# Dilated sliding attention and a squared-ReLU FFN on one core: the order of the first batch, other homes for copies and products, and the last tile in two banks

## The chip, the core and the metric

One core of one Trainium2 chip. The metric is the device time of one launch in microseconds, as the median of several runs: 314.54 us for the kernel before (13 runs, 313.2 to 317.0). The profile is of one execution of 314.25 us. Engines: PE is TensorE, DVE is VectorE, ACT is ScalarE, POOL is GpSimd and SP is SyncE. POOL and SP issue transfers here; ACT issues a few at the start.

## The reference

q, k and v have 8 batches, 8 heads, 576 positions and 64 features. Heads 0 to 3 see the last 32 positions. Heads 4 to 7 see those of the last 128 whose distance is a multiple of 4.

```python
scores = scale * np.matmul(q, k.transpose(0, 1, 3, 2))
rel = pos[:, None] - pos[None, :]
mask_plain = (rel >= 0) & (rel < window)
mask_dil = (rel >= 0) & (rel < window * dilation) & (rel % dilation == 0)
...
attn = attn / (np.sum(attn, axis=-1, keepdims=True) + 1e-09)
...
x = np.ascontiguousarray(attn_out.transpose(0, 2, 1, 3)).reshape(B * S, H * D)
h = np.maximum(x @ w_in, 0.0)
return (h * h @ w_out).astype(np.float32)
```

The FFN takes all 4608 tokens from 512 features to 2048 and back.

## The kernel before, in words

**FFN.** It is cut into tiles of tokens: four of 256, then seven of 512. A tile consists of groups of products. A group of the first layer (`mm1`, L655) multiplies quarters of w_in with the transposed attention output xT into a bank of PSUM (L665); ACT applies ReLU into h2T (L676) and DVE squares it (L677). A group of the second layer (`g2`, L692) adds four products of 128 tokens with a quarter of w_out (L700); after the fourth, ACT copies the bank into osb (L706) and SP stores it. Of the last 128 tokens of all, each half of the columns is finished, copied and stored by itself (L696 to L698), both halves in one bank. The first two 512-token steps' products are cut once more by heads (`g1`, L679), so that they can start before the last head pair is ready. FFN groups are numbered from 0 over the whole kernel.

**Attention.** Two heads form a pair, e = 0 to 3; pairs 0 and 1 are the plain ones, 2 and 3 the dilated ones. For each batch and pair, q and k have to be transposed. In batches 0, 1 and part of 2, PE transposes them into PSUM (`trans`, L221, products at L235), and copies (`halves`, L240; L248 for q, L252, L259 and L265 for k) bring them to qT and kbd: four copies for each q or k, two for each head. kbd holds two heads as blocks on a diagonal, so one product does both. Later batches are transposed by transfers (`cross`, L213), and the same copies take them from SBUF. v is spread into vbd by transfers or by DVE (`spread_v`, L202). `scores` (L295) makes products of kbd and qT, ACT takes the exponential (L314), DVE multiplies by the mask (L315). `pv` (L342) multiplies with vbd (L413) and with ones for the sums (L415); ACT makes the reciprocal as logarithm and exponential (L417, L418), and DVE multiplies into xT (L428). PSUM has four banks in pool pf for the FFN, two in pa, and one each in po and pd. Products of batches 0 and 1 with e odd go to pf, all others to po and pd.

**The order** is written by hand in `PROGRAM` (L21). What stands ahead of the first `|` is done before FFN group 0; after FFN group n, the codes of the (n+1)-th part that follows are done. I call that slot n. Slots hold codes of batches 1 to 5; the rest follows a rule. A code such as `1q2` is batch, step and pair. q and k transpose and copy, Q and K do it for a batch's second part (positions from 256 on), v and V spread v, a and b are the two halves of scores, o and p the two halves of products. `L` codes load, and `L3:x` is the transposing transfer.

The first batch has steps of its own (`first_step`, L471), with pair and part as digits: T transposes, C copies (L504 to L512), B adds the mask's bias to PSUM, S the scores (L546), E the exponential (L554) and, in the second part (x1), the mask (L557), P the products with v (L584), D the sums (L600), L and X the reciprocal (L607, L610), M the product into xT (L617). W with a number issues that many products of an idle tile on PE (L467, `turn`).

Of the kernel before, what the change touches and what calls it, by code (L numbers as in the profile page):

```python
# [20 lines left out]
PROGRAM = (  # L21
    "L0:q001 L0:q023 L0:q101 L0:q123 L0:v0d L0:i0 L0:v1dr L0:i1 L0:v1p L0:i2 L0:i3 L0:o0 L0:o1 L0:o2 L0:o3 "
    "L1:q00123 z y L1:v0dp L1:q10123 L1:v1dpr w9 T00 C00a T10 C10a B00 B10 W2 S00 E00 B20 W1 S10 E10 u B30 W3 "
    "T20q W6 T20k C20v T30 C30v h W3 S20 E20 W2 S30 E30 T01 C01v T11 C11v W2 P00 P10 D00 D10 L00 X00 M00 P20 "
    "P30 D20 D30 L20 X20 M20 S01 T21 C21a T31 C31v E01 S11 E11 | S21 E21 | S31 E31 P21 P31 D21 D31 L21 X21 M21 "
    "L31 X31 M31 | | P01 P11 D01 D11 L01 X01 M01 L11 X11 M11 | | | | | | | | | | | | | m n | | | | | L2:q00123 "
    "L2:q10123 | 1q1 1q3 | 1q2 1k2 | 1k1 1v3 | 1a2 | 1v2 1k0 1q0 | 1o2 | 1a0 1a1 | 1k3 1o0 1o1 | 1a3 1Q0 | 1K0 "
    "1o3 | 1Q1 1K1 | 1Q2 | 1b0 | | 1Q3 1K2 L2:vwpdr L3:q00123 L3:q10123 | L2:x | | 2q0 | | 2k0 1V2 | 1b2 1p0 | "
    "1b1 1V3 1K3 | | 1p2 1p1 | 2a0 1b3 | 2k1 2o0 2b0 1p3 | 2q1 2k2 L3:x | | 2q2 2p0 L3:vwpdr 2a1 | | | 2b1 | "
    "2o1 2q3 2a2 | | 2p1 2v2 | 2k3 | 2b2 2o2 | 2v3 | 2a3 2p2 L4:q10123 | 2b3 3k1 | 2o3 3q1 | | 3a1 L4:q00123 "  # L30
    "2p3 | 3k0 3k2 | | 3o1 | | | 3q0 3v2 | | | | 3a0 | 3b1 3k3 | | | 3p1 L4:x 3q2 L4:vwpdr | | 3b0 | 3a2 3q3 "
    "3o0 4k0 | | | 3o2 3b2 | | 3p0 3v3 | 4q1 3a3 | 3p2 4q2 4q0 | L5:q10123 3b3 | 3o3 | 4k1 | | L5:q00123 3p3 "
    "4k2 4k3 4a0 L5:vwpdr | | | 4b0 | | 4q3 | | 4o0 | | | 4a2 4v2 | 4b2 | 4a3 L5:x 4a1 | 4o2 | | | 4p2 "
    "L6:q00123 4v3 | | 4b1 | | 4p0 | | 4p1 | 5q0 5k0 | 4b3 | | | | 4o1 | | 5k2 L6:q10123 4o3 | 5q2 5k1 | | 4p3 "
    "| 5q1 |"
)


# [25 lines left out]
def kernel(  # L64
# [9 lines left out]
    nc = tc.nc  # L74
    P = nc.NUM_PARTITIONS
    B, H, S, D = q.shape
    DM, DFF = moe_w_in.shape
    NTOK = B * S
    assert H * D == DM
    bf16 = mybir.dt.bfloat16  # L80
# [5 lines left out]
    NE = H // 2  # L86
# [3 lines left out]
    M = S // RES  # L90
# [5 lines left out]
    PARTED = (0, 1)  # L96
    STAGE = (0, 1, 0, 2, 2, 2, 0, 1)
    ADDED = 4
# [12 lines left out]
    ps_f = ctx.enter_context(tc.tile_pool(name="ps_f", bufs=4, space=bass.MemoryType.PSUM))  # L111
    ps_a = ctx.enter_context(tc.tile_pool(name="ps_a", bufs=2, space=bass.MemoryType.PSUM))
# [37 lines left out]
    def staged(b: int, nm: str):  # L150


        t = rb[STAGE[b]][nm]
        return t[:, :].rearrange("p (a h x) -> p a h x", h=H, a=2)
# [47 lines left out]
    def spread_v(b: int, e: int, parts):  # L202

        p0, p1 = parts[0], parts[-1] + 1
        for hl in range(2):
            rows = slice(64 * hl, 64 * hl + 64)
            nc.vector.tensor_copy(  # L207
                vbd[b % 2][rows, e, RES * p0 : RES * p1, rows],
                vds[b][rows, e - NE // 2, p0:p1, :].rearrange("p m (r d) -> p (m r) d", d=D),
            )  # L210
# [7 lines left out]
            staged(b, nm)[0:n, part, h0:, :].rearrange("p h x -> p (h x)"),  # L218
        )

    def trans(b: int, e: int, nm: str, part: int):  # L221

        ps = ps_a.tile([P, 1024], bf16, name="pa")
        t = staged(b, nm)
        copy = nc.scalar.copy if nm == "q" and e < NE // 2 else nc.vector.tensor_copy
        if b == 2:
            m0, n, pitch, cuts = 0, M, M, [(t[0:80, a, :, :], MS[a], 80) for a in range(2)]
        else:

            m0, n, pitch, cuts = MS[part], MN[part], 80, [(t[0:80, part, :, :], 0, 80)]  # L230
        pv_ = ps[:, 0 : 4 * pitch].rearrange("p (h c m) -> p h c m", h=2, c=2)
        for hl in range(2):
            for c in range(2):
                for src, c0, w in cuts:
                    nc.tensor.transpose(  # L235
                        pv_[:, hl, c, c0 : c0 + w], src[:, 2 * e + hl, P * c : P * c + P], ident[0:w, 0:w]
                    )
        halves(e, nm, pv_[:, :, :, 0:n], m0, n, copy)

    def halves(e: int, nm: str, t, m0: int, n: int, copy):  # L240


        for hl in range(2):
            rows = slice(64 * hl, 64 * hl + 64)
            for jj in range(2):
                src = t[64 * jj : 64 * jj + 64, hl, :, :]
                if nm == "q":
                    copy(  # L248
                        qT[rows, e, :, m0 : m0 + n].rearrange("p (c j) m -> p j c m", j=2)[:, jj, :, :], src
                    )  # L250
                elif e < NE // 2:
                    copy(  # L252
                        kbd[rows, e, m0 // 16 : (m0 + n) // 16, rows].rearrange(
                            "p i (m c j) -> p j i m c", c=2, j=2)[:, jj, :, :, :],
                        src.rearrange("p c (i m) -> p i m c", m=16),
                    )
                else:
                    x0, x1 = m0 // 64, min((m0 + n) // 64, 2)
                    copy(  # L259
                        kbd[rows, e, RES * x0 : RES * x1, rows].rearrange(  # L260
                            "p (x c j) m -> p j c x m", c=2, j=2)[:, jj, :, :, :],
                        src[:, :, 0 : 64 * (x1 - x0)].rearrange("p c (x m) -> p c x m", m=64),
                    )
                    if m0 + n == M:
                        copy(  # L265
                            kbd[rows, e, 8, rows].rearrange("p (m c j) -> p j m c", c=2, j=2)[:, jj, :, :],
                            src[:, :, n - 16 : n].rearrange("p c m -> p m c"),
                        )
# [163 lines left out]
    def step(b: int, code: str):  # L432

        what, e = code[0], int(code[1])
        part = int(what in "QKVbp")
        if what in "qk" and (b > XB or b == XB and e >= NE // 2):
            t = (qx if what == "q" else kx)[b % 2]
            by_act = what == "q" and e < NE // 2 and b < ADDED  # L440
            halves(
                e, what, t[:, 2 * e : 2 * e + 2, :, :], 0, M, nc.scalar.copy if by_act else nc.vector.tensor_copy
            )
        elif what in "qQkK":
            trans(b, e, what.lower(), part)
        elif what in "vV":
            spread_v(b, e, [part] if b in PARTED else [0, 1])
        elif what in "ab":
            scores(b, e, part)
        elif b in PARTED and e % 2:  # L450
            pv(b, e, part, ps_f, "pf")
        else:
            pv(b, e, part)
# [175 lines left out]
    def store(osb, pos: int, c0: int = 0, c1: int = DM):  # L629

        x = 0
        while x < P:
            b, y = divmod(pos + x, S)
            part = int(y >= RES * MN[0]) if b in PARTED else 0
            w = MN[part] if b in PARTED else M
            r, m = divmod(y - RES * MS[part], w)
            n = min(P - x, w - m)
            row = b * S + RES * (MS[part] + m) + r
            nc.sync.dma_start(out[row : row + RES * (n - 1) + 1 : RES, c0:c1], osb[x : x + n, c0:c1])
            x += n  # L640

    def ffn_groups(tk0: int, nt: int):
# [3 lines left out]
        early = NT <= tk0 <= 2 * NT  # L646
# [43 lines left out]
                mm1(i, kts)  # L690

        def g2(m, part):  # L692
            if part == 0:
                cur[m] = ps_f.tile([P, DM], f32, name="pf")

            last = tk0 + P * (m + 1) == NTOK  # L696
            c0, c1 = (DM // 2 * (part // 2), DM // 2 * (part // 2 + 1)) if last else (0, DM)
            f0, f1 = (NF // 2 * (part % 2), NF // 2 * (part % 2 + 1)) if last else (4 * part, 4 * part + 4)  # L698
            for f in range(f0, f1):
                nc.tensor.matmul(  # L700
                    cur[m][:, c0:c1], h2[:, f, P * m : P * m + P], w_out_sb[:, f, c0:c1],
                    start=(f == 0), stop=(f == NF - 1),
                )
            if f1 == NF:
                osb = osb_pool.tile([P, DM], f32, name="osb")
                nc.scalar.copy(osb[:, c0:c1], cur[m][:, c0:c1])  # L706
                store(osb, tk0 + P * m, c0, c1)

        return [lambda i=i: g1(i) for i in range(NF // per)] + [
            lambda m=m, part=part: g2(m, part) for m in range(nt // P) for part in range(4)  # L710
        ]

# [163 lines left out]
```

## Time and profile before

| | |
|---|---|
| median of 13 runs | 314.54 us (313.2 to 317.0) |
| the profiled execution | 314.25 us, span 312.5 us |
| mean granted clock of PE | 0.995 |
| FFN, first layer (L665) | 768 products, 135.0 us busy |
| FFN, second layer (L700) | 592 products, 134.5 us busy |
| h2T square on DVE (L677) | 144, mean 423 ns |
| ReLU on ACT (L676) | 144, mean 597 ns |

Start and length stand first in a row of the timeline, then engine, line, operation, output and inputs. Busy time of PE overlaps from product to product, since ends are modelled, so late starts are found by the difference of starts. Slots come in time order: slot 22 is at 41.9 us, slot 64 at about 93.9 us.

### The profile page before, as it was taken

How to read it: one execution, taken by the hardware profiler on the slowest of the kernel's cores; microseconds unless marked ns; L12 is line 12 of the kernel's file. 1: busy time of each engine (PE TensorE's matmuls, PEld its weight loads, DVE VectorE, ACT ScalarE, POOL GpSimd, SP SyncE). 2: the span in 40 equal slices, each digit the busy share in tenths (PEclk: the TensorE clock that was granted, in tenths of full speed). 3: DMA queues.
4: the chain of work that ended last, by engine and by line, in shares of the span. 5: the costliest groups of instructions: out<-in, count | busy, mean ns of one | idle time of the engine just before them, and what ended most of it. 6: DMA issues, size and time to landing. Idle time of an engine off the chain costs nothing.

```text
span 312.5 us, 6788 instructions
## 1 busy us (share of the span) xinstructions
PE 303.9 (97%) x2564; PEld 187.4 (60%) x2564; DVE 196.0 (63%) x637; ACT 197.6 (63%) x421; POOL 94.0 (30%) x138
## 2 busy tenths in 40 slices
PE   8989999999999999999999999999999999999994
PEld 4669746968755555555599655555555555445443
DVE  1446568898987879985799469946994334104400
ACT  6658638759878956785388547854686456226511
POOL 8679788626083127401451041000000000000000
PEclk9979999999999999999999999999999999999999
DMA  7999999999999899995699975602200210121022
GB/s 107 196 183 215 199 153 185 196 158 200 142 133 205 110 186 140 142 183 69 93 130 129 163 121 94 103 8 61 67 3 0 69 68 0 36 67 34 2 67 67
DMA packets 79808, 35.04 MB, mean 112 GB/s; under 512 B 49824, under 2 KB 74784, under 8 KB 79776
## 3 DMA queue, kind: packets, MB, share of 16 engines
q0 software_dynamic: 46592, 18.23, 51.0%
q1 hardware_dynamic: 32496, 16.06, 26.4%
q10 hardware_dynamic: 688, 0.33, 0.5%
q8 instruction: 20, 0.33, 0.4%
q14 instruction: 12, 0.10, 0.1%
HBM read 36.90 MB, written 9.44 MB: 148 GB/s over the span
## 4 chain that ended last, share of the span: by engine, by line
PE 85%; ACT 5%; DMA 4%; DVE 2%; issue 2%; POOL 0%; ACTq 0%; POOLq 0%
PE pf L665 38%; PE pf L700 37%; PE po L413 3%; DMA w_in<-in_moe_w_in_dram 3%; PE pd L415 2%; DMA qb<-in_q_dram 2%; PE pa L304 2%; ACT h2T L676 1%; PE pa L310 1%; ACT qT L248 1%; PE pa L235 1%; ACT rec L417 1%; DVE kbd L252 1%; DVE xT L428 1%; ACT rec L418 1%
## 5 line engine op out<-in xcount | busy, mean ns | idle before, releaser
L665 PE MATMUL pf<-xT,w_in 128*128 128x256 bf16 (+1 forms) x768 | 135.0, 328 | 0.9 <-DVE xT L428 0.3
L700 PE MATMUL pf<-w_out_sb,h2T 128*128 128x512 bf16 (+1 forms) x592 | 134.5, 373 | 0.5 <-ACT osb L706 0.5
L665 PEld LDWEIGHTS <-w_in 128*128 128x128 bf16 x768 | 82.7, 114 | 36.9 <-issue 1.2
L676 ACT ACTIVATE h2T<-pf 128x512 bf16<-128x512 f32 x144 | 83.7, 597 | 23.5 <-PE pf L665 22.9
L700 PEld LDWEIGHTS <-h2T 128*128 128x128 bf16 x592 | 54.3, 98 | 54.0 <-issue 0.7
L677 DVE TENSOR_TENSOR h2T<-h2T 128x512 bf16<-128x512 bf16 x144 | 58.0, 423 | 38.7 <-ACT h2T L676 37.1
L706 ACT COPY osb<-pf 128x512 f32<-128x512 f32 (+1 forms) x37 | 21.2, 573 | 43.5 <-PE pf L700 41.3
L428 DVE TENSOR_TENSOR xT<-po,rec 128x288 bf16<-128x288 f32 (+2 forms) x52 | 23.7, 456 | 31.5 <-ACT rec L418 31.0
L178 POOL DMA_DIRECT2D vbd<-in_v_dram x36 | 25.7, 729 | 54.2 <-PE pd L415 49.4
L417 ACT ACTIVATE rec<-pd 128x288 f32<-128x288 f32 (+2 forms) x52 | 21.5, 413 | 24.0 <-PE pd L415 22.9
L314 ACT ACTIVATE pt<-pa 128x352 bf16<-128x352 f32 (+6 forms) x56 | 27.6, 499 | 8.4 <-PE pa L310 4.7
L418 ACT ACTIVATE rec<-rec 128x288 f32<-128x288 f32 (+2 forms) x56 | 24.8, 444 | 1.8
L413 PEld LDWEIGHTS <-vbd 128*128 128x128 bf16 x286 | 16.8, 97 | 10.0 <-DVE vbd L207 0.7
L248 DVE COPY qT<-xx 64x288 bf16<-64x288 bf16 x80 | 19.6, 246 | 1.1
L161 POOL DMA_DIRECT2D qb<-in_q_dram x18 | 13.0, 721 | 21.8 <-DMA xx<-qb 19.6
L252 DVE COPY kbd<-xx 64x288 bf16<-64x288 bf16 x40 | 18.8, 470 | 0.6
L413 PE MATMUL po<-pt,vbd 128*128 128x96 bf16 (+3 forms) x263 | 18.0, 199 | 0.3 <-DVE vbd L207 0.2
L191 POOL DMA_DIRECT2D vd<-in_v_dram x24 | 14.7, 630 | 6.4 <-DMA kb<-in_k_dram 2.6
L415 PE MATMUL pd<-pt,mk 128*128 128x96 bf16 (+5 forms) x158 | 16.3, 204 | 0.0
L161 POOL DMA_DIRECT2D kb<-in_k_dram x18 | 12.8, 712 | 0.4 <-issue 0.3
L304 PE MATMUL pa<-qT,kbd 128*128 128x96 bf16 (+2 forms) x146 | 12.2, 201 | 0.5 <-ACT qT L248 0.5
L197 POOL DMA_DIRECT2D vbd<-in_v_dram x16 | 9.6, 606 | 9.4 <-PE pd L415 7.4
(90 smaller groups left out, 236.7 us busy)
## 6 DMA issues: line engine op xcount, KB each, us to landing
out_dram<-osb SPq DMA_DIRECT2D x18, 128.0 KB, 4.5
qb<-in_q_dram POOLq DMA_DIRECT2D x7, 320.0 KB, 7.7
kb<-in_k_dram POOLq DMA_DIRECT2D x7, 320.0 KB, 9.0
vd<-in_v_dram POOLq DMA_DIRECT2D x32, 64.0 KB, 4.8
w_in<-in_moe_w_in_dram POOLq DMA_DIRECT2D x4, 512.0 KB, 7.8
w_out_sb<-in_moe_w_out_dram POOLq DMA_DIRECT2D x4, 512.0 KB, 11.4
qb<-in_q_dram POOLq DMA_DIRECT2D x7, 256.0 KB, 6.2
kb<-in_k_dram POOLq DMA_DIRECT2D x7, 256.0 KB, 7.5
```

Source lines behind the costliest of these rows:

```text
L161: nc.gpsimd.dma_start(t[0:n, part, hs, :], src[b, hs, t0 : t0 + RES * n, :].rearrange("h (p r) d -> p h (r d)", r=RES))
L178: nc.gpsimd.dma_start(dst[rows, e, i0:i1, rows], v[b, 2 * e + hl, 64 * i0 : 64 * i1, :].rearrange("(i p) d -> p i d", p=64),)
L248: copy(qT[rows, e, :, m0 : m0 + n].rearrange("p (c j) m -> p j c m", j=2)[:, jj, :, :], src)
L314: nc.scalar.activation(pt[:, off : off + n], ps[:, 0:n], ACT.Exp, scale=SCALE)
L413: nc.tensor.matmul(oo, vb[:, e, i, :], rh, start=(x == 0), stop=(x == len(mms) - 1), skip_group_check=True)
L417: nc.scalar.activation(rec[:, 0:n], d[:, 0:n], ACT.Ln)
L418: nc.scalar.activation(rec[:, 0:n], rec[:, 0:n], ACT.Exp, scale=-1.0)
L428: nc.vector.tensor_tensor(out=tok, in0=o if o is o3 else o[:, 0:n], in1=rec if o is o3 else rec[:, 0:n], op=ALU.mult)
L665: nc.tensor.matmul(acc[u][:, nt * x + y0 : nt * x + y1], w_in_sb[piece][:, kt, c0 : c0 + 509 : 4], xT[:, kt, t0 : t0 + y1 - y0], start=(kt ...
L676: nc.scalar.activation(hv, acc[u][:, :].rearrange("p (x n) -> p x n", x=per), ACT.Relu)
L677: nc.vector.tensor_tensor(out=hv, in0=hv, in1=hv, op=ALU.mult)
L700: nc.tensor.matmul(cur[m][:, c0:c1], h2[:, f, P * m : P * m + P], w_out_sb[:, f, c0:c1], start=(f == 0), stop=(f == NF - 1),)
```

## The change

`PROGRAM` has another order in the first batch. The first batch's `T21 C21 T31 C31` move from after S01 to between L00 and X00. S21, S31, E21 and E31, which stood in and behind slots 0 and 1, and S01, S11, E01, E11 all stand before FFN group 0 now, E21 and E31 first. C11 has its q copied by ACT, C21 by DVE. W2 ahead of P00 becomes W4.

```diff
-C20v T30 C30v h W3 S20 E20 W2 S30 E30 T01 C01v T11 C11v W2 P00 P10 D00 D10 L00 X00 M00 P20
-P30 D20 D30 L20 X20 M20 S01 T21 C21a T31 C31v E01 S11 E11 | S21 E21 | S31 E31 P21 P31 D21 D31 ...
+C20v T30 C30v h W3 S20 E20 W2 S30 E30 T01 C01v T11 C11a W4 P00 P10 D00 D10 L00 T21 C21v T31
+C31v X00 M00 P20 P30 D20 D30 L20 X20 M20 S21 S31 E21 E31 S01 S11 E01 E11 | | P21 P31 D21 D31 ...
-L2:q10123 | 1q1 1q3 | 1q2 1k2 | 1k1 1v3 | 1a2 | 1v2 1k0 1q0 | 1o2 | 1a0 1a1 | 1k3 1o0 1o1 | ...
+L2:q10123 | 1q1 1q3 | 1q2f 1k2f | 1k1a 1v3 | 1a2 | 1v2 1k0a 1q0v | 1o2 | 1a0 1a1 | 1k3 1o0 1o1f | ...
-1b1 1V3 1K3 | | 1p2 1p1 | 2a0 1b3 | 2k1 2o0 2b0 1p3 | 2q1 2k2 L3:x | ...
+1b1 1V3 1K3 | | 1p2 1p1f | 2a0 1b3 | 2k1l 2o0 1p3f 2b0 2k1h | 2q1 2k2 L3:x | ...
-2o1 2q3 2a2 | | 2p1 2v2 | 2k3 | 2b2 2o2 | 2v3 | 2a3 2p2 L4:q10123 | 2b3 3k1 | 2o3 3q1 | | 3a1 L4:q00123 2p3 | 3k0 3k2 | | 3o1 | | | 3q0 3v2 |
+2o1 2a2 2v2 2q3 | | 2p1f | 2k3 | 2b2 2o2 | 2v3 | 2a3 2p2f L4:q10123 | 2b3 2o3 | 3k1 | 2p3 | 3q1v L4:q00123 | 3k0l | 3a1 | 3k0h | | 3o1 3k2l | 3q0 | 3k2h 3v2 |
```

A code may now end in its home: `f` puts its PSUM into pool pf, `a` and `v` have its copies done by ACT or DVE, `l` does the first head's two copies and `h` the second head's later. Products go to pf only with an `f`: of those that went there before, 1o3 goes to po and pd now. New are 2p1 and 2p2 in pf.

```diff
-    def trans(b: int, e: int, nm: str, part: int):
-        ps = ps_a.tile([P, 1024], bf16, name="pa")
+    def trans(b: int, e: int, nm: str, part: int, home: str):
+        pool, name = (ps_f, "pf") if "f" in home else (ps_a, "pa")
+        ps = pool.tile([P, 1024], bf16, name=name)
         t = staged(b, nm)
-        copy = nc.scalar.copy if nm == "q" and e < NE // 2 else nc.vector.tensor_copy
+        copy = copier(nm, e, home, True)
...
+    def copier(nm: str, e: int, home: str, early: bool):
+        act = "a" in home or "v" not in home and nm == "q" and e < NE // 2 and early
+        return nc.scalar.copy if act else nc.vector.tensor_copy
...
-        elif b in PARTED and e % 2:
+        elif "f" in home:
             pv(b, e, part, ps_f, "pf")
```

In the last tile, the second half of the columns takes a bank of its own:

```diff
         def g2(m, part):
-            if part == 0:
+            last = tk0 + P * (m + 1) == NTOK
+            if part == 0 or last and part == 2:
                 cur[m] = ps_f.tile([P, DM], f32, name="pf")
```

## The prediction

> **What bounds the kernel now.** I read the page first: busy shares, then the tenths with the clock row.
>
> ```profile
> PE 303.9 (97%) x2564; PEld 187.4 (60%) x2564; DVE 196.0 (63%) x637; ACT 197.6 (63%) x421; POOL 94.0 (30%) x138
> ...
> PE   8989999999999999999999999999999999999994
> ...
> PEclk9979999999999999999999999999999999999999
> ```
>
> TensorE (PE) is never long idle, and from 126 us to 306 us no group of its products starts late. A gain can only come from late starts of PE and from its clock. So I went through the PE timeline with the price of one product: in the chain, 13.81 us for 64 products of 512 columns gives 0.216 us each, and 10.48 us for 96 of 256 columns gives 0.109 us. Where the next start is later than that, PE stood still. These late starts are in three places.
>
> The head. Stages of 3.4 us, columns as in the first line (PE, PEld, DVE, ACT, POOL, clock, DMA share, GB/s), then the chain of waits:
>
> ```profile
> 12.92:16.34 3.42, 2.64 (x75) 2.01 (x76) 1.58 (x3) 3.09 (x6) 2.22 (x4) 1.00 1.31 194
> 16.34:19.75 3.41, 3.41 (x32) 2.31 (x32) 1.74 (x7) 1.50 (x4) 3.30 (x5) 0.50 1.56 187
> 19.75:23.16 3.41, 2.60 (x66) 2.21 (x65) 1.34 (x4) 2.03 (x4) 1.97 (x5) 1.00 1.29 179
> ```
>
> ```profile
> 8.25 7.91 DMA w_in<-in_moe_w_in_dram
> 16.16 0.05 issue
> 16.21 1.83 PE pf L665 x8
> 18.04 0.67 PE pf L546 x9
> 18.71 0.99 PE pf L665 x4
> ...
> 20.75 0.60 ACT pt L554
> 21.35 0.02 issue
> 21.37 0.44 DVE pt L557
> ...
> 21.85 0.59 PE pa L584 x14
> ```
>
> The first weights land at 16.16 us, then FFN groups 0 and 1 run at half clock, then the chain goes over the exponential (L554) and mask (L557) of heads 6 and 7, second part. The third FFN group starts at 22.72 us. The same stretch has 0.89 us in which PE waits for the values (12.71 to 13.60).
>
> The middle. Lines from the PE timeline; the bracket is the idle time before and its releaser:
>
> ```profile
> 43.37 0.30 PE L235 MATMUL pa<-mk,qb 80*128 80x80 bf16 x4 [0.15 <-ACT qT L248]
> ...
> 54.85 0.82 PE L665 MATMUL pf<-xT,w_in 128*128 128x256 bf16 x6 [0.25 <-ACT osb L706]
> ...
> 93.89 0.32 PE L304 MATMUL pa<-qT,kbd 128*128 128x96 bf16 x4 [0.45 <-ACT qT L248]
> ...
> 96.13 1.02 PE L665 MATMUL pf<-xT,w_in 128*128 128x512 bf16 x4 [0.27 <-DVE xT L428]
> ```
>
> The bracket is shorter than the loss, since the modelled ends overlap it. Start to start, less the price of the product, the losses after 40 us are: 0.32 (ends 43.37), 0.18 (44.7), 0.25 (46.9), 0.19 (49.4), 0.42 (54.8), 0.17 (62.3), 0.25 (76.1), 0.26 (83.5), 0.36 (86.2), 0.62 (93.9), 0.43 (96.1), 0.20 (120.6): 3.6 us.
>
> The tail:
>
> ```profile
> 306.48 0.37 ACT L706 COPY osb<-pf 128x256 f32<-128x256 f32 x1 [1.16 <-PE pf L700]
> 306.90 1.91 PE L700 MATMUL pf<-w_out_sb,h2T 128*128 128x256 bf16 x16 [0.51 <-ACT osb L706]
> ```
>
> The last tile's second half waits until ScalarE (ACT) has copied the first half out of the same bank: start to start 0.78 us where 0.11 is due.
>
> **The head, part by part.** W4 for W2 is two more dummy products of 256 columns: 2 x 0.109 = 0.2 us later for P00, P10 and their sums D00, D10, which then end near 13.1. T21 and T31 (32 transposes, 0.8 us by the rows at 14.69 to 15.5) move ahead of P20, into the old wait for the values: they end near 13.8, so P20 starts 0.15 us after those values have landed (it began at 13.30 and 13.65), and ends with its sums at 14.6. VectorE (DVE) now takes C21 and C31 (0.48 + 0.21 us each) from 13.5 to 14.9, so M00 behind them moves from 14.23 to 14.9 and ends at 15.6: it is due at 16.2, so nothing is lost. The copy of T11 by ACT (L511) costs 0.3 us where ACT stood idle (1.41 us before L607). PE then has S21 and S31 (0.5 us each), S01 and S11 (0.3 each) until about 16.3; ACT has, after its reciprocals (to 15.9), E21, E31 (0.6 each), E01, E11 (0.5 each), to 18.1. The accumulators of FFN group 0 are the banks that E21 and E31 free at 16.5 and 17.1: groups 0 and 1 start at 16.5, not at 16.2. Their 16 products end at 18.4 at full clock, at 19.9 at half clock. Masks for heads 4 to 7 are done by then, so P21, P31, D21, D31 (1.3 us from the rows 20.47 to 20.84 and 21.85 to 22.7) follow without the old 0.98 us stop before 21.85, and end at 19.7 or 21.2. The third FFN group needs the second quarter of the weights, issued at 13.22 and landing 7.8 us later, at 21.00. So it starts at 21.05 or 21.2 in place of 22.72: **-1.6 us**, nearly the same at either clock. What is late next: the third quarter (landed 24.28) is due at 24.5, the fourth (27.33) near 30.7, the last quarter of w_out (37.21) near 38.4; all hold.
>
> Here a rule has to be weighed. The Trainium skill, "TensorE: Matmul & The Clock Gate", Part 1, has the clock fall after an idle window of about 3.4 us. The row 12.92:16.34 says otherwise: PE was busy for 2.64 of 3.42 us and the next window still had half clock, while 19.75:23.16, no busier (2.60), kept full clock. By the rule the change would get 18.4 for groups 0 and 1; by the row, with some 0.4 us less idle and 36 more small products in that window, either may come. The sum takes the row, and the weights' landing makes both ends equal to 0.15 us.
>
> **Batch 1 (slots 22 to 35).** The transposes 1q2 and 1k2 go to two of the four banks of pool pf. Those two last held accumulators that ACT read long before, so 1q2 needs no bank of 1q1 and the 0.32 goes. k of pair 1 and 0 is copied by ACT, q of pair 0 by DVE: 8 copies of L252 (0.30 us each on DVE) leave DVE, 4 of L248 (0.22) come. A kbd copy by ACT is nowhere in the trace. Nearest row: ACT's L248 for the same 64x128 takes 0.27 (1.08 for four); the wider L252 on DVE takes 0.47. I take 0.27 to 0.30; the ends are 0.22 and 0.47, worth -0.2 and +0.8 us on each of two chains of four copies. From the start of slot 22 as zero, before had 1a2 at 3.8, 1a0 at 7.55 and 1o3 at 11.7 us; walking the new order with these durations gives 1a2 at 3.5 (q2 and k2 by DVE end at 3.45), 1a0 at 6.7, 1o0 at 8.2 (ACT is now busy with an output copy and a reciprocal ahead of that exponential), 1o3 at 11.0. That gains 0.66, and the 0.42 at 54.8 goes, because one pair of products fewer sits in pf and the late accumulator takes its bank 2.6 us later: **-1.0 us** of 1.36. The product 1o3 moves to the single pair po, pd, which frees 0.9 us before it is due. The 0.17 at 62.3 stays.
>
> **Batches 2 to 4 (slots 45 to 72).** Splitting 2k1 puts two copies (2 x 0.49 us) behind 1p3's product into xT; it frees its bank 0.98 us earlier, and 0.25 goes. 2p1 in pf does not wait for po: 0.26. 2v2 two slots earlier: 0.36. For 3a1, count from T, the end of FFN group 61: DVE does 2o3's product to T+2.5, four copies of 3k1 (0.47 each) to T+4.4, 2p3's product to T+4.9, four of 3q1 (0.25) to T+5.9. Group 66 wants 2p3's result at T+5.2, so the 0.43 goes; 3a1 comes at T+5.6 and waits 0.3, where it was 0.62. Together 0.25 + 0.26 + 0.36 + 0.43 + 0.3 = 1.6. 3q1 is 1.0 us more on DVE in a stretch that was 90% busy (100:110); its last h2T product was ready 1.7 us before its use at 108.5, so it covers that with 0.7 left; without it this costs up to 1.0. I book 0.3 for new small waits: **-1.3 us**. The 0.20 at 120.6 stays.
>
> No load, transposing transfer or store changes place in POOL's or SP's order. PE now runs up to 4 us ahead of transfers which do not move: the tightest is batch 1's first q (landed 38.96, due at 40.3 after the head's gain), then batch 2's q (56.25 against 58.9) and k.
>
> **Tail.** The second half gets its own bank, long free. PE goes on at once, ACT's 0.37 us copy lies under 16 products: 0.78 - 0.11 less some issue, **-0.55 us**. Least nothing, most 0.67.
>
> **Sum.** 1.6 + 1.0 + 1.3 + 0.55 = 4.45 us off the profiled execution's own 314.25 (span 312.5): 309.8. That execution was 0.29 us under the median of the runs, 314.54, so as a median: 310.1 us.
>
> **Rivals.**
> - The middle gives nothing: the copies are the chain whatever their bank, and PE, ahead, meets the next one. For it: DVE is 90% busy at 60 to 70 and 100 to 110. Against: each loss has its own named releaser. Then 1.6 + 0.55: 312.4. Chance 0.16.
> - The clock falls once more. In the new order PE can idle from 19.7 to 21.0, for the weights. If the window after has half clock over dense FFN products, half of 3.4 us is lost: 310.1 + 1.7 = 311.8. Against: 19.75:23.16 had 0.8 us idle and kept it. Chance 0.10.
> - No change: new waits eat what is won, or the head's gain is given back at batch 1, because loads land later than in this execution (margin 1.3 us). 313 to 316. Chance 0.10.
> - Slower: kbd copies by ACT, strided in the output, take far longer than any row. Two chains of four stand before 1a2 and 1a0, so each 0.1 us more costs 0.8 us. It decides from 0.27 + 4.45 / 8 = 0.83 us; at 1.1 us the time is 310.1 + 6.6 = 316.7. Against: no copy of that width is over 0.3. Chance 0.06.
>
> The forecast itself has 0.58 and its own range is 308.8 to 311.4. The low end takes every saving in full (1.75 + 1.36 + 1.9 + 0.65 = 5.7, at 308.8); the range goes to 312.6 to take in the first two rivals, which leaves about 0.16 outside. A measurement of this kernel tells some 0.5%, 1.6 us, from no change. Faster by more: 0.58 + 0.16 + 0.10 = 0.84.
>
> **What would show it.** The third FFN group (L665 in before's numbering, on w_in's second quarter) at 21.0 to 21.3; no PE stop before 43.4, 54.9, 83.5 and 86.2; one of about 0.3 us for 3a1; four ACT copies into kbd of about 1.1 us twice; no PE gap behind the first half of the last tile. Wrong if the second quarter of w_in lands after 22, if kbd copies on ACT are over 0.5 us, or if the stretch 98 to 110 shows h2T waited for by PE.

## The result and the profile after

The changed kernel takes 310.46 us as the median of 11 runs (309.61 to 311.62). The kernel before, run beside it, takes 314.46 us (48 runs, 312.72 to 317.43). The ratio is 0.988, with an interval from 0.985 to 0.990. The profiled execution took 309.38 us (span 307.6), against 314.25 (span 312.5): 4.87 us less. Lines of the changed kernel are 8 above those of before from `halves` on: L673 is the first FFN layer, L708 the second, L592 the first batch's product with v. In `trans` they are 1 above (L236). In `middle_only`, `better`, `better2` and the kernels `after_...` other than `after_again`, every such line is one more (L674, L237).

First the page: the busy line, the tenths of PE and its clock.

```profile
PE 300.8 (98%) x2566; PEld 187.0 (61%) x2566; DVE 195.8 (64%) x637; ACT 196.6 (64%) x421; POOL 93.9 (31%) x138
...
PE   8899999999999999999999999999999999999995
...
PEclk9999999999999999999999999999999999999999
```

The third digit of the clock row is 9 where it was 7: in this execution PE had full clock throughout. That by itself is a warning, since the profiled execution of before had 3.4 us at half clock. So I read where the time went by the starts of the same FFN product in both traces (product 0 is the first of L665 / L673; there are 1360). The difference between two neighbouring rows is what a stretch gained.

| FFN product | what begins there | before, us | after, us | difference |
|---|---|---|---|---|
| 0 | group 0 | 16.21 | 17.33 | +1.12 |
| 16 | third group | 22.72 | 20.62 | -2.11 |
| 128 | first of the second layer | 35.85 | 33.75 | -2.11 |
| 256 | after batch 1's slots | 62.59 | 59.35 | -3.24 |
| 288 | | 73.57 | 70.44 | -3.13 |
| 320 | | 78.21 | 75.06 | -3.15 |
| 352 | | 82.44 | 79.29 | -3.15 |
| 384 | | 91.98 | 88.71 | -3.27 |
| 448 | | 108.51 | 104.09 | -4.43 |
| 512 | after batch 4's slots | 125.79 | 121.58 | -4.20 |
| 1343 | last of the last tile's first half | 306.12 | 301.92 | -4.20 |
| 1344 | first of its second half | 306.90 | 302.03 | -4.87 |

From 126 to 302 us nothing changed, to 0.01 us. The gain is made in the three places where PE had started late: 2.11 in the head, 1.13 in batch 1, 0.96 in batches 2 to 4, 0.67 in the tail.

The head, in stages of the same width and columns as before (us, PE, PEld, DVE, ACT, POOL busy, clock, DMA share, GB/s):

```profile
12.92:16.34 3.42, 2.19 (x96) 1.77 (x91) 1.84 (x5) 1.79 (x4) 2.08 (x3) 1.00 1.33 195
16.34:19.75 3.41, 2.76 (x53) 2.42 (x47) 2.44 (x6) 3.21 (x7) 2.83 (x5) 1.00 1.49 181
19.75:23.16 3.41, 3.41 (x62) 3.27 (x62) 1.87 (x5) 2.73 (x7) 3.33 (x7) 1.00 1.16 160
```

And its chain of waits:

```profile
6.89 7.80 DMA vd<-in_v_dram
14.70 0.04 issue
14.74 0.43 PE po L592 x15
...
16.80 0.49 ACT pt L562
17.29 0.04 issue
17.33 1.96 PE pf L673 x16
19.29 0.52 PE po L592 x17
19.82 0.52 PE pa L592 x17
```

The values of heads 4 and 5 (vd) landed at 14.70 here, not at 13.60, and group 0 starts 1.1 us later than before, held by an exponential (L562). Still the third group is earlier: the products P21 and P31 (L592) now follow groups 0 and 1 without any stop, where before had the exponential and the mask between them. PE stood still there for 0.98 us from start to start, in this row of before:

```profile
21.85 0.46 PE L584 MATMUL pa<-pt,vd 64*64 64x32 bf16 x16 [0.81 <-DVE pt L557]
```

The third group's first product starts at 20.62.

The middle, from the PE timeline:

```profile
40.95 0.31 PE L236 MATMUL pf<-mk,qb 80*128 80x80 bf16 x4
...
50.92 1.47 PE L673 MATMUL pf<-xT,w_in 128*128 128x256 bf16 x12
...
91.97 0.32 PE L312 MATMUL pa<-qT,kbd 128*128 128x96 bf16 x4
```

None of the three has the bracket of an idle time any more (it was 0.15, 0.25 and 0.45 us). From start to start, the third (the scores 3a1) is still 0.23 us late, where it was 0.62. And the tail, from ACT's timeline and from PE's:

```profile
302.28 0.37 ACT L714 COPY osb<-pf 128x256 f32<-128x256 f32 x1 [1.16 <-PE pf L708]
304.02 0.37 ACT L714 COPY osb<-pf 128x256 f32<-128x256 f32 x1 [1.38 <-PE pf L708]
```

```profile
299.64 4.30 PE L708 MATMUL pf<-w_out_sb,h2T 128*128 128x512 bf16 x35
```

PE runs as one row across both halves; ACT's copy of the first half at 302.28 lies under the second half's products.

### The profile page after: what moved, and what is told of

It reads as the page before. It is cut to its first block, busy times and chain, and to the rows that moved or that the text cites. A ratio compares the mean times of both kernels' runs of the same rounds, so it can differ in the third digit from the quotient of the medians.

```text
span 307.6 us, 6794 instructions
## 1 busy us (share of the span) xinstructions
PE 300.8 (98%) x2566; PEld 187.0 (61%) x2566; DVE 195.8 (64%) x637; ACT 196.6 (64%) x421; POOL 93.9 (31%) x138
## 4 chain that ended last, share of the span: by engine, by line
PE 91%; DMA 3%; POOL 2%; ACT 2%; DVE 1%; issue 1%; ACTq 0%; POOLq 0%
PE pf L708 40%; PE pf L673 39%; PE po L421 3%; DMA vd<-in_v_dram 3%; PE pd L423 2%; PE pa L312 2%; PE pa L318 2%; PE pa L236 1%; POOL qb L161 1%; POOL kb L161 1%; DVE kbd L260 1%; ACT rec L425 1%; ACT rec L426 0%; DVE qT L256 0%; PE po L592 0%
## 5 line engine op out<-in xcount | busy, mean ns | idle before, releaser
L708 PE MATMUL pf<-w_out_sb,h2T 128*128 128x512 bf16 (+1 forms) x592 | 134.2, 373 | 0.0
L673 PE MATMUL pf<-xT,w_in 128*128 128x256 bf16 (+1 forms) x768 | 133.1, 326 | 0.6 <-ACT pt L562 0.6
L673 PEld LDWEIGHTS <-w_in 128*128 128x128 bf16 x768 | 82.3, 114 | 35.2 <-issue 0.5
L708 PEld LDWEIGHTS <-h2T 128*128 128x128 bf16 x592 | 54.3, 98 | 53.5
L256 DVE COPY qT<-xx 64x288 bf16<-64x288 bf16 x84 | 21.0, 250 | 1.1
L421 PE MATMUL po<-pt,vbd 128*128 128x32 bf16 (+3 forms) x256 | 17.5, 198 | 0.0
L423 PE MATMUL pd<-pt,mk 128*128 128x32 bf16 (+6 forms) x150 | 15.9, 204 | 0.0
```

What stands on the lines that cost most here:

```text
L421: nc.tensor.matmul(oo, vb[:, e, i, :], rh, start=(x == 0), stop=(x == len(mms) - 1), skip_group_check=True)
L423: nc.tensor.matmul(dd, ones[:, :], rh, start=(x == 0), stop=(x == len(dms) - 1), skip_group_check=True)
L673: nc.tensor.matmul(acc[u][:, nt * x + y0 : nt * x + y1], w_in_sb[piece][:, kt, c0 : c0 + 509 : 4], xT[:, kt, t0 : t0 + y1 - y0], start=(kt ...
L708: nc.tensor.matmul(cur[m][:, c0:c1], h2[:, f, P * m : P * m + P], w_out_sb[:, f, c0:c1], start=(f == 0), stop=(f == NF - 1),)
```

## The experiments

The theory is the prediction's: three independent sets of late starts are removed, each by its own part. The rivals are that the head's gain is the clock only (before had a half-clock window in its profile), that the middle gives nothing, and that the copies of k by ACT cost more than they save. In tables of stretches, "128 to 640" is the time from FFN product 128 to 640.

### One part alone: head, middle, tail

Three kernels, each the kernel before with one part of the change. `head_only` takes only the text ahead of the third group:

```diff
-... T11 C11v W2 P00 P10 D00 D10 L00 X00 M00 P20
-P30 D20 D30 L20 X20 M20 S01 T21 C21a T31 C31v E01 S11 E11 | S21 E21 | S31 E31 P21 P31 ...
+... T11 C11a W4 P00 P10 D00 D10 L00 T21 C21v T31 C31v X00 M00 P20
+P30 D20 D30 L20 X20 M20 S21 S31 E21 E31 S01 S11 E01 E11 | | P21 P31 ...
```

> The kernel before with only the first batch's new order. Theory (four separate savings that add up): the third FFN group starts about 2 us earlier (20.6 to 21.2 in place of 22.7) and the whole is 1.6 to 2.1 us shorter, about 312.6. Rival (PE, ahead, only meets the same copies and loads later): the third group is earlier, but the gain is gone by slot 40, and the time is within 0.7 us of before. In runs in which one 3.4 us window has half clock the time should be 1.7 us longer, here as in before.

`middle_only` has the other homes and slots from slot 3 on, with the first batch and the last tile of before:

```diff
-... | 1q2 1k2 | 1k1 1v3 | 1a2 | 1v2 1k0 1q0 | ... | 3q0 3v2 |
+... | 1q2f 1k2f | 1k1a 1v3 | 1a2 | 1v2 1k0a 1q0v | ... | 3q0 | 3k2h 3v2 |
```

> The kernel before with only the new homes and slots of batches 1 to 4 (first batch and last tile as before). Theory: late starts of PE between 40 and 126 us fall from 3.6 us to some 1.3, and the time falls by 2.1 us to about 312.4. Rival (the middle's late starts shrink only because the head gives the copies another timing against the loads): less than 1 us.

`tail_only` has only the second bank:

```diff
-            if part == 0:
+            last = tk0 + P * (m + 1) == NTOK
+            if part == 0 or last and part == 2:
```

> The kernel before with only the last tile's second half in its own bank. Theory: the start to start step across the halves falls from 0.78 to 0.11 us, so 0.67 us in the profile, about 313.8; under what the timed runs can tell. Rival (the last store is what ends the kernel, and it waits for the queue): PE ends earlier but the span stays.

| | median us (n) | ratio and interval | third group at, us | 128 to 640, us | 1343 to 1344, us |
|---|---|---|---|---|---|
| before | 313.90 (35) | 1 | 22.72 | 121.67 | 0.78 |
| head_only | 312.96 (12) | 0.9968 [0.9942, 0.9994] | 21.20 | 121.59 | 0.78 |
| middle_only | 313.00 (12) | 0.9962 [0.9930, 0.9994] | 24.59 | 120.21 | 0.78 |
| tail_only | 313.05 (12) | 0.9961 [0.9935, 0.9987] | 22.16 | 121.60 | 0.11 |
| after | 310.46 (11) | 0.9876 [0.9849, 0.9902] | 20.62 | 119.57 | 0.11 |

(The last three columns are from one profiled execution each; the row "after" was timed on another occasion.) Every part's edit shows in its own stretch. Where another stretch differs too, as the third group of `tail_only` and `middle_only` does, it lies ahead of the edit. The parts' ratios give 0.32 + 0.38 + 0.39 = 1.09%, the whole 1.24%: they add up within their intervals. The runs with a clock of 0.998 or more alone have medians of 313.64 (before, 22 runs), 312.82 (head, 10), 311.34 (middle, 4) and 312.59 us (tail, 9): 0.8, 2.3 and 1.05 us less. The tail's 1.05 is more than the 0.67 of its stretch, so 0.4 us of such a difference may be chance. The head alone was expected to give 1.6 to 2.1 us and the middle alone 2.1; both gave 0.9 in the medians of all runs. So the rival "the middle gives nothing" falls, and so does "the head's gain is given back at batch 1": 21.20 is still a lead of 1.5 us at product 128 and at 512 (34.36 and 124.23 against 35.85 and 125.79).

The middle alone gains 1.46 in its stretch, not 2.10 as in the whole. Behind the old head the slots come later in relation to their inputs, and two late starts of 0.36 and 0.41 us are left at 110, both for copies of q by DVE (L257).

Its third group is late for a reason that stands ahead of its first edited slot, and which the head's stages show:

```profile
12.92:16.34 3.42, 1.49 (x24) 0.90 (x24) 1.11 (x3) 1.26 (x3) 2.35 (x4) 0.66 1.30 190
16.34:19.75 3.41, 3.41 (x62) 2.83 (x61) 2.07 (x6) 2.85 (x5) 2.54 (x5) 0.50 1.47 185
```

The values landed at 14.84 in this execution, PE idled 1.9 us for them, and the clock was halved for 6.8 us, from 14.0 to 20.8. Seven of its twelve runs had a mean clock of 0.993 or less and took 313.0 to 316.1 us; the four at 0.998 or more took 311.15 to 311.61. Of the 35 runs of before only 4 were at 0.993 or less; why this kernel has more of them is not shown. So the median of `middle_only` understates its part, and the question of the clock has to be asked by itself.

### Is the head's gain only the clock?

`before_filled` is the kernel before with eight idle products in the wait for the values, so that PE does not fall idle there:

```diff
-P00 P10 D00 D10 L00 X00 M00 P20
+P00 P10 D00 D10 L00 W8 X00 M00 P20
```

> The kernel before with eight idle products of 256 columns (0.87 us) put into PE's wait for the values ahead of P20; nothing else is changed. Rival theory of the head: its gain is the clock, since before's profile had one window at half clock and after's had none. Then the filler alone keeps the clock, and 1 to 1.7 us are gained, near 313. Theory (the order gains, by taking the exponentials and masks of heads 6 and 7 from PE's path): the third FFN group still waits for the mask behind S31, so the gain is 1 us or less, and without a half clock window in the profile it starts at 21.5 or later.

Measured: 314.08 us (12 runs, 312.79 to 314.79), ratio 0.9979 [0.9952, 1.0006]; the 22 runs of before with the same clock have a median of 313.64, so the filler gains nothing. The clock was 0.998 or higher in all 12 runs; the stages of the head show what the filler does.

```profile
12.92:16.34 3.42, 3.27 (x78) 2.62 (x80) 1.79 (x5) 1.85 (x4) 2.90 (x5) 1.00 1.30 183
16.34:19.75 3.41, 3.28 (x76) 2.68 (x72) 2.41 (x7) 3.17 (x7) 2.36 (x5) 1.00 1.36 185
```

PE has 3.27 us of work where it had 2.64, the clock is kept, and yet the third group starts at 22.20. The chain of this kernel says why:

```profile
17.17 1.06 PE pf L665 x8
18.23 0.44 PE pf L546 x18
...
18.69 0.60 ACT pt L554
19.29 0.85 ACT h2T L676 x2
...
20.22 0.61 ACT pt L554
...
20.86 0.44 DVE pt L557
...
21.34 0.59 PE pa L584 x14
```

Scores, two exponentials with two ReLUs between them, mask, product: this chain holds PE at full clock too. From the first FFN product to the third group the old order takes 5.03 us here and 5.04 in `tail_only` (both at full clock) and 6.51 in the profile of before; the new one takes 3.29 in the profile of after and 3.63 in `head_only`. So the clock accounts for up to 1.5 us of an execution in which it falls, but the order wins another 1.4 to 1.7 in this stretch at full clock on both sides. Part of that is spent ahead of it, since group 0 starts later. Set against `tail_only` (22.16), the third group is 0.96 us earlier in `head_only` and 1.54 in the profile of after. The rival falls as the only cause.

### Where the middle's gain sits

Two kernels take back one half each of batch 1's edit. `after_k_by_dve` gives the copies of k and q back to the engines that had them:

```diff
-1k1a 1v3 | 1a2 | 1v2 1k0a 1q0v
+1k1 1v3 | 1a2 | 1v2 1k0 1q0
```

> The changed kernel, but k of batch 1's pairs 1 and 0 copied by DVE and q of pair 0 by ACT, as before the change (1q2 and 1k2 stay in pf). One look at the stretch from FFN product 160 to 192 (10.13 us before, 9.69 after). Theory (each late start has a chain of copies of its own, and sharing 1k1 and 1k0 between engines took 0.18 + 0.25 + 0.19 us away): it is 0.3 to 0.6 us longer than after's. Rival (the bank of 1q2 and 1k2 was the only cause, the later ones followed from it): it stays within 0.1 us of after's.

One run: 310.38 us. The stretch 128 to 192 takes 17.79 us in it, 17.17 in the changed kernel and 17.93 in the one before: undone, this edit alone costs 0.62. The rows of both engines price the copy that no trace of before had, first ACT in the changed kernel, then DVE in this one:

```profile
42.44 1.23 ACT L260 COPY kbd<-pa 64x128 bf16<-64x128 bf16 x4 [0.62 <-PE pa L236]
44.54 1.23 ACT L260 COPY kbd<-pa 64x128 bf16<-64x128 bf16 x4 [0.46 <-PE pa L236]
```

```profile
43.45 1.24 DVE L261 COPY kbd<-pa 64x128 bf16<-64x128 bf16 x4
44.72 0.72 DVE L208 COPY vbd<-vd 64x256 bf16<-64x256 bf16 x2
...
46.14 1.24 DVE L261 COPY kbd<-pa 64x128 bf16<-64x128 bf16 x4
```

Four copies take 1.23 us on ACT and 1.24 on DVE. Neither is faster. What is gained is the queue: on DVE the copies stand one after another without a gap, and the spread of v (L208) and the mask come late behind them. PE shows it, in the same kernel:

```profile
46.17 0.29 PE L422 MATMUL po<-pt,vbd 128*128 128x64 bf16 x4 [0.26 <-DVE vbd L208]
```

`after_q2_in_pa` puts the transposes of q2 and k2 back into pool pa:

```diff
-1q2f 1k2f
+1q2 1k2
```

> The changed kernel, but 1q2 and 1k2 transposed into pa as before. One look. Theory: 1q2 waits again for the bank of 1q1 until ACT has copied it, and the step from product 144 to 160 is 0.32 us longer than after's 4.03. Rival (the bank is free in time, since PE is earlier relative to nothing in that slot): unchanged.

One run: 310.34 us; 128 to 192 takes 17.57, so 0.40 more. The two costs, 0.62 and 0.40, exceed the stretch's whole gain of 0.76 (17.93 less 17.17): with the other edit missing, the bank gains only 0.14 and the copies 0.36. So the two are not separate savings. Both old waits are back at once:

```profile
41.92 0.30 PE L237 MATMUL pa<-mk,qb 80*128 80x80 bf16 x4 [0.16 <-ACT qT L257]
43.24 0.32 PE L237 MATMUL pa<-mk,kb 80*128 80x80 bf16 x4 [0.23 <-DVE qT L257]
```

For batches 2 to 4, `after_three_undone` undoes three edits that lie far enough apart to be read separately:

```diff
-2k1l 2o0 1p3f 2b0 2k1h
+2k1 2o0 1p3f 2b0
-2p1f
+2p1
-3q1v
+3q1
```

> The changed kernel with three edits of batches 2 to 4 undone, which lie in different stretches: 2k1 copied in one piece ahead of 1p3's product, 2p1 in po, q of 3q1 copied by ACT. One look, read by stretches of FFN products. Theory (each has its own late start): 288 to 320 is 0.2 us longer, 320 to 384 0.25 us, and 384 to 400 0.3 to 0.6 us longer, while 400 to 480 gets 0.2 us shorter, since DVE is 1.0 us freer. Rival (the new slots alone do it): less than 0.2 us in sum.

One run: 311.59 us; its head had a late transfer of w_in, so only the stretches count.

| stretch | edit undone | before | after | after, again | undone |
|---|---|---|---|---|---|
| 288 to 320 | 2k1 in two pieces | 4.64 | 4.62 | 4.63 | 4.40 |
| 352 to 384 | 2p1 in pf | 9.54 | 9.42 | 9.42 | 10.04 |
| 384 to 448 | 3q1 by DVE | 16.54 | 15.38 | 15.39 | 15.18 |

The new order moves attention products out of 384 to 400 into both neighbours, so before compares with after only over 352 to 448 together: 26.07 against 24.80 us.

Two of my three forecasts fail. Splitting 2k1 gains nothing: undone, the stretch is 0.22 shorter, while eight traces with the split all show 4.62 or 4.63. The 0.25 us that 1p3 waited were gone in the changed kernel, but the transposes of 2q1 behind it wait for their bank about as long (0.24 us, until 71.99): the split keeps 2k1's own bank taken until its second head is copied.

Copying 3q1 by DVE is not what removes the wait of 3a1 either: by ACT it stays gone. What removes it lies among the new slots (3a1 later, 2o3 and 2p3 earlier), which no run took apart. Whether 3q1 on DVE costs the 0.21 us of the table is not shown: `after_q2_in_pa` and `middle_only` have it on DVE too and take 15.21 and 15.18. What differs is how long its four copies take, since 3a1 starts behind the last of them. The first row is of the changed kernel, where 3a1 is 0.23 us late, the second of `middle_only`, where it is not late:

```profile
90.49 1.43 DVE L256 COPY qT<-xx 64x288 bf16<-64x288 bf16 x4
```

```profile
94.75 0.95 DVE L257 COPY qT<-xx 64x288 bf16<-64x288 bf16 x4
```

A late start of 0.19 us at 106 in the changed kernel, which DVE's additional work could have explained, stays without it (at 108.3).

2p1 in pf, on the other hand, is worth 0.62, not 0.25. In po it waits until DVE has read the product before it out of that bank (first row, 0.36 us late from start to start), and the next product into po starts 0.40 us late again (second row):

```profile
82.19 0.39 PE L422 MATMUL po<-pt,vbd 128*128 128x32 bf16 x6 [0.19 <-DVE xT L437]
...
84.91 0.33 PE L422 MATMUL po<-pt,vbd 128*128 128x96 bf16 x5 [0.23 <-DVE xT L437]
```

The second row is the start for which the prediction booked 0.36, to be won by the earlier slot of 2v2. That slot was kept here, so without 2p1 in pf it does not win it.

### Filling the head, and a better order

In the changed kernel PE still waits 1.2 us for the values and 0.6 us for E21, the first of the exponentials at L562. `after_filled` puts idle products in both places:

```diff
-X00 M00 P20 P30 ... E01 E11 | |
+X00 M00 W3 P20 P30 ... E01 E11 W6 | |
```

> The changed kernel with idle products put into the two stops that its head still has: three ahead of P20 (wait for the values) and six ahead of FFN group 0 (wait for the exponentials' bank). Theory (after's runs are split by one window of half clock, which comes when the window before it holds too little work of PE): all runs keep a granted clock of 0.998 or more, and the median falls by 0.3 to 0.8 us from 310.46 to about 309.9, the lowest runs staying where they are. Rival (the split is the transfers' doing): the granted clock and the spread stay, and the median is the same or 0.3 us worse for the filler.

Measured: 311.12 us (6 runs, 310.1 to 311.71), ratio 0.9894 [0.9855, 0.9934]. The clock was 0.998 or more in all six, but the median did not fall to 309.9. Idle products go to bank po, and there they wait until DVE has read the first batch's products out of it (the row's releaser):

```profile
17.80 0.82 PE L476 MATMUL po<-idle 128*128 128x256 bf16 x6 [0.89 <-DVE xT L626]
18.45 1.80 PE L674 MATMUL pf<-xT,w_in 128*128 128x256 bf16 x15
```

Group 0 starts at 18.45 us in place of 17.33: the filler itself was the stop. `after_filled2` lets the six products add zeros into S11's bank, ahead of its exponential:

```diff
-S01 S11 E01 E11
+S01 S11 W6+11 E01 E11
```

> The changed kernel with idle products again, but those ahead of FFN group 0 added (as zeros) into the bank of S11, so that they do not have to wait for po as in the first try, where they held group 0 up by some 0.8 us. Theory: group 0 starts with E31, as in after (near 17.3); granted clock 0.998 or more in all runs; median 309.7 to 310.1, against 310.2 to 310.6 for the changed kernel. Rival (the transfers split the runs, not the clock): no difference.

Measured: 310.22 us (6 runs, 309.84 to 311.69), ratio 0.9874 [0.9826, 0.9923], clock 0.998 or more in all six. The 309.7 to 310.1 expected is missed, and the timed runs do not tell this kernel from the changed one. PE goes through without a stop and group 0 is not delayed:

```profile
16.63 0.83 PE L476 MATMUL pf<-idle 128*128 128x256 bf16 x6
17.34 1.96 PE L674 MATMUL pf<-xT,w_in 128*128 128x256 bf16 x16
```

Two kernels tried to go on from the stretches. `better` is the first filler with 2q0 and 2q1 in pf, 3p2 in pf, 3a1 one slot later and 3q2 one slot earlier; `better2` is the second filler with 2q0 and 3p2 in pf and 3q2 earlier:

```diff
-2q0 | ... 2q1 2k2 ... 3k0l | 3a1 | 3k0h | ... | | 3p1 L4:x 3q2 ... 3p2
+2q0f | ... 2q1f 2k2 ... 3k0l | | 3a1 3k0h | ... | 3q2 | 3p1 L4:x ... 3p2f
```

> The same with five of the late starts that after still shows in the middle taken on: 2q0 and 2q1 transposed into pf, 3p2 in pf, 3a1 one slot later, 3q2 one slot earlier. Theory: 58.8 (0.15), 71.7 (0.23), 91.5 (0.24), 106.1 (0.19) and 116.0 (0.20) go, 0.7 to 0.9 us in the profile, median about 309.1. Rival (a late start that goes comes back at the next step that needs the same engine): at most 0.3 us.

```diff
-2q0 | ... | | 3p1 L4:x 3q2 ... 3p2
+2q0f | ... | 3q2 | 3p1 L4:x ... 3p2f
```

> That with three edits which gained in the first try: 2q0 in pf (0.16), 3q2 one slot earlier and 3p2 in pf (0.36 together); 2q1 stays in pa and 3a1 in its slot, since those lost 1.0 and 0.46. Theory: 0.5 us more than the filler alone in the profile's stretches from 192 on, median near 309.3. Rival: the late starts move and under 0.2 us is left.

`better`: 311.48 us (6 runs, 311.24 to 312.25), ratio 0.9911 [0.9876, 0.9947], a miss. Putting 2q1 in pf takes a bank that the FFN needs next, and the copies of 2q1 on ACT become its wait:

```profile
75.99 1.25 PE L674 MATMUL pf<-xT,w_in 128*128 128x256 bf16 x10 [1.03 <-ACT qT L257]
```

288 to 320 takes 5.60 us in place of 4.63, and with 3a1 a slot later a product behind it starts 0.48 us late, start to start, because DVE's mask of 3a1's exponentials (L324) is not ready. `better2` leaves both out: 310.25 us (6 runs, 309.58 to 313.31), ratio 0.9881 [0.9830, 0.9932]. In its profile 192 to 256 takes 8.29 in place of the 8.42 of `after_again` and 448 to 512 takes 17.15 in place of 17.38, some 0.4 us together (six traces of the changed order take 17.37 to 17.64 in the second). The timed runs cannot tell that from the changed kernel.

### The changed kernel once more

`after_again` is the changed kernel itself, timed beside `after_three_undone`, `after_filled2` and `better2` on one chip.

> The changed kernel as it is, for a comparison on the same chip with the two above. Theory: about 310.4, in a third of the runs a granted clock of 0.995 or less and 1 to 1.7 us more; without half clock 309.4 to 310.3. Rival: the runs spread as much at full clock, so that the landing of the first weights and values sets the spread.

Measured: 310.60 us (6 runs, 309.52 to 312.41), ratio 0.9883 [0.9836, 0.9930]. The two runs with a clock of 0.994 took 310.84 and 312.41 us. In the profiled one the clock was full, and still its third group came at 22.46. The end of its head's chain:

```profile
13.78 8.63 DMA w_in<-in_moe_w_in_dram
22.41 0.05 issue
22.46 1.94 PE pf L673 x16
```

The second quarter of w_in landed at 22.41 us, where it landed at 20.11 in the other profile of the same kernel. PE stopped for 1.0 us ahead of it. From product 128 to 448 the two profiles agree within 0.02 us in every stretch; 448 to 512 takes 17.38 against 17.49 us.

## Why the prediction held

The prediction said 310.1 us and the runs gave 310.46; on profiled executions the sum was 4.45 us and the traces give 4.87. By its own steps:

- **The head (-1.6; measured -2.11).** P21 and P31 follow groups 0 and 1 without the stop, as forecast. What then sets the third group's start is not what the prediction said. It had the second quarter of w_in land at 21.00 and set the start; the quarter landed at 20.11, and PE's own chain ended later. The values landed at 14.70 instead of 13.60, so P20 waited 1.2 us in place of 0.15; the reciprocals and E21 came behind it, group 0 started at 17.33 in place of 16.5, and 3.29 us of products later the third group at 20.62. Of the five traces with exactly this head (`after`, `after_again`, `after_k_by_dve`, `after_q2_in_pa`, `after_three_undone`) four take the same 3.28 or 3.29 us and are set by this chain; only `after_again` (landing 22.41) is set by w_in, as is `head_only` (21.16). That the size came near is partly luck: a late chain met an early landing, and the execution of before that served as baseline had half clock. Against the old order at full clock (22.16 in `tail_only`) the trace gains 1.54, and `head_only` 0.96. That the third quarter of w_in holds came out in the profile of after, but two traces waited for it: 16 to 128 takes 13.13 us there, 14.07 in `after_q2_in_pa` and 14.82 in `after_three_undone`.
- **Batch 1 (-1.0; measured -1.13).** Copies of k by ACT took 0.298 us where I took 0.27 to 0.30. Taking back the copies costs 0.62, taking back the bank 0.40; their gains overlap, so the terms cannot be priced one by one.
- **Batches 2 to 4 (-1.3; measured -0.96).** The terms that concern 83 to 98 us (0.26, 0.36, 0.43 and 0.3, together 1.35) measured 1.27 over the products 352 to 448. The 0.3 booked for new waits measured 0.33 net over all other stretches but 2k1's. What failed is the step "Splitting 2k1 ... it frees its bank 0.98 us earlier, and 0.25 goes": it measured 0.02, since the next transposes wait in its place. The step on 3a1 forecast a rest of 0.3 us late and the trace has 0.23, but which of its edits does it was not separated, only that 3q1 by DVE is not needed.
- **The tail (-0.55; measured -0.67).** I had taken something off for issue; there was nothing to take off, 0.78 became 0.11.

Of the rivals, "the middle gives nothing" and "slower through ACT's copies" are refuted by `middle_only` and by the 0.298 us. "The clock falls once more" is no either-or: it happened in 4 of 12 runs of the changed kernel, counting the profiled one, which had full clock (0.994 in the four, 310.98 to 311.62 us, median 311.58, against 309.9 in the seven at 0.998 or more). That is the price of 1.7 us that I gave it. I treated it as a case of 1 in 10; it comes and goes from run to run. I had also expected PE to idle less in the window before group 0; it was busy for 2.19 us of it instead of 2.64, so the full clock in the profile is luck. The kernel before pays it too: of the 35 runs beside the first experiments, 13 at 0.996 or less have a median of 315.27 and 22 at 0.998 or more one of 313.64. At full clock on both sides, then, the change is worth 313.64 - 309.9 = 3.7 us, though the two were timed on different occasions. Side by side on one chip, six such runs of before (313.2) and four of `after_again` (310.2) differ by 3.0. So the gain does not rest on the clock, but at full clock it is 3.0 to 3.7 us rather than 4.4.

What stays open: what decides whether a window's work counts as enough to keep the clock (below), and whether 2k1 in one piece together with the edits of `better2` would add up to the 0.6 us that their stretches promise (0.22 + 0.4). That kernel was not run. Of batches 2 to 4, only the three edits above were undone singly; the other new slots, 2p2 in pf and the splits of 3k0 and 3k2 were not.

## What to carry to other kernels

Where PE is the bound and 97% busy, list its late starts one by one, by differences of starts, and name the releaser of each; edits in separate parts of the kernel add up here, two edits of one chain of copies did not, and whether one really gained is read in the stretch around it, since a wait that is removed may only let the next instruction meet the same queue. Moving a copy to another engine pays by the queue that it leaves, not by its own duration: here the copy took the same 0.3 us on both. A filler product needs a bank that nobody is reading, or it becomes the stop.

## What the runs showed of the hardware

- **The clock does not follow PE's busy time in the window.** The prediction weighed a rule of the Trainium skill, "TensorE: Matmul & The Clock Gate", Part 1 (the clock falls after an idle window), against before's row of 2.64 us busy that was followed by half clock. The row decides against it here: PE was busy for 77% of that stage. The runs give no threshold either. This stage of `better` was followed by half clock:

```profile
12.90:16.31 3.41, 2.54 (x67) 1.71 (x66) 2.00 (x6) 1.26 (x3) 2.28 (x4) 1.00 1.29 189
16.31:19.72 3.41, 3.32 (x67) 2.83 (x64) 2.07 (x5) 3.08 (x6) 2.10 (x4) 0.50 1.41 177
```

  while the changed kernel, with 2.19 us in the stage above, kept full clock. That does not hang on where the stages are cut: however its head is cut into stages of 3.41 us, one of them holds at most 2.47 us of PE work. Filling the wait helps without being certain: 34 of the 36 runs with a filler had 0.997 or more, one of `better` 0.994 and one of `better2` 0.995.
- **The landing of the same load moves by over 2 us between executions.** The second quarter of w_in took 7.2 us from issue to landing in one execution of the changed kernel and landed 2.3 us later in another. The later one's third group is 1.84 us later, and its profiled execution 1.75 us longer. With the clock at 0.998 or more, `before_filled` still spread from 312.79 to 314.79 us; what spreads it was not traced.
- **A copy of 64x128 from PSUM into the interleaved columns of kbd costs the same on ACT as on DVE.** Four in a row took 1.23 and 1.24 us above, though the plain copy of q is dearer on ACT (busy us, mean ns; groups of the changed kernel, shapes kept apart):

```profile
L260 ACT COPY kbd<-pa 64x128 bf16<-64x128 bf16 x8 | 2.4, 298 | 1.2 <-PE pa L236 1.1
...
L256 DVE COPY qT<-pa 64x128 bf16<-64x128 bf16 x8 | 1.8, 222 | 1.6 <-PE pa L236 1.5
...
L256 ACT COPY qT<-pa 64x128 bf16<-64x128 bf16 x4 | 1.0, 260 | 0.5 <-PE pa L236 0.4
```

- **A copy on DVE from SBUF to SBUF can take more than twice as long while POOL issues a transfer.** Such a copy of q (64x288) took 0.22 to 0.25 us in 803 of 916 cases in eleven traces. The other 113 took up to 0.60, and every one of them ended 0.02 to 0.06 us after POOL had ended an issue. This is what made the four copies of 3q1 take 0.95 us in one execution and 1.43 in another.
